# A two-layer decode kernel with 27 unit buffers in place of 26, and 22 kept units of each row in place of 20

## The chip, the cores and the metric

The kernel runs on one core of a Trainium2 chip. The metric is the device time of one execution in microseconds, the median of several. The profile is one further execution; its span, from the first to the last instruction, is 1 to 2 us shorter than the device time.

## The reference

Eight sequences (rows), one new token each, pass through two rounds of attention and MLP. Both rounds use the same weights and the same caches, so a layer-1 query reads the same keys and values as the layer-0 query of its row.

```python
def _A_ref(x, k_cache, v_cache, wq, wo):      # x: 8 x 1 x 640, caches: 8 x 32 x 4096 x 128
    W = min(4096, max(256, Sk // 4))          # the last 1024 positions
    q = (x @ wq) as 32 heads of 128
    k, v = k_cache[:, :, Sk - W:], v_cache[:, :, Sk - W:]
    p = softmax(q k^T * Dh ** -0.5)
    return (p v as 4096 columns) @ wo
def _B_ref(x, w1, b1, w2, b2):                # 640 -> 1728 -> 640
    y = layernorm(x)
    return gelu(y @ w1 + b1) @ w2 + b2
x = x + _A_ref(layernorm(x), ...)             # layer 0
x = x + _B_ref(layernorm(x), ...)
x = x + _A_ref(layernorm(x), ...)             # layer 1
x = x + _B_ref(layernorm(x), ...)
```

All tensors are bfloat16. The used part of the caches is 134 MB[...]; weights are another 15 MB.

## The kernel before

**Units.** A unit is the keys, or the values, of one pair of heads of one row: 128 partitions x 2048 bf16, 512 KB, fetched by one DMA from the SyncE queue (`load`, L357). A row has 16 pairs, so 32 units. `NUNIT = 26` unit buffers hold them. A buffer is free again when the last matmul on it is done (`release`).

**Stream and keep.** In layer 0 each row reads all its 32 units. Pairs 6 to 15 (KEEP, three jobs of 2, 4 and 4 pairs) stay in their 20 buffers until layer 1 of the same row has used them; pairs 0 to 5 (STREAM, two jobs "a" and "b" of 3 pairs) are read and dropped, and read again for layer 1. While a row's 20 kept units wait for its layer-1 query, 6 buffers are left for streams.

**A job** is a set of pairs of one row and layer. Its steps, with the engine and the line in the profile: `expand` puts the queries into a weight with zeros around them (VectorE, L367); `scores`, four matmuls of 512 columns for each unit of keys, on four column groups of the array (TensorE, L377); `exponent` (ScalarE, L386) into the row `p`; `turn`, four small matmuls that transpose p (L392); `place` copies the result among zeros into a `pv` buffer (ScalarE, L400); `totals` and `inverse` give the softmax sums (L405, L409, L411); `values`, four matmuls for each unit of values (L419), into an `o` bank of PSUM; `fold` (four times, L431 and L433) and `halve` (twice, L441 and L443) bring the wanted blocks together in `acc` and `parts`; `gathered` (L448) turns them into columns; `finish` (L475) scales them. In layer 0 `project` (L488) multiplies with wo into the attention bank of PSUM, 5 matmuls of one column for each head, in groups of 15 or 20. In layer 1 `finish` writes the output into the SBUF table `qo`, and all rows are projected together at the end (`gather`, L676). The last job of a row's layer 0 takes values unit by unit into columns (`columns`, L459) in place of values, fold and gather.

**The chain of a row.** When all projections of row b are done, `chain` runs the first MLP for that row alone: add (L608), layer norm (L247 to L272, its root on GpSimd, L264), `hidden` (14 chunks of w1, L300), bias and tanh, `gate` (L317), `outer` (14 chunks of w2, L329), another layer norm, and then the queries of layer 1 (`query`, L619; L623 copies those that are not used at once into `qo`). During this chain the queue streams the jobs of `WINDOWS[b]`: pairs that layer 0 of later rows and layer 1 of earlier rows need. As layer 1 of row b releases its kept units, the kept units of row b + 1 are loaded.

**Order.** Loads stand in a fixed list (`add_loads`): keys of a job and values of the job before it by turns. All instructions of all engines are emitted in the order of the string `ORDER`, which picks at each step one of the tasks left, and which was found by a search over planned durations (the second argument of `plan.add`). `Plan` checks counts of shared things: unit buffers, 2 score banks `s`, 3 query buffers `qz`, 1 row `p`, 2 buffers `pv`, 2 banks `o`, 1 pair `acc` and `parts` (`f`), 3 small banks `c`, 5 `rd`. The waits themselves are put in by the framework from what each instruction reads and writes; it keeps engines apart in a PSUM bank.

**Ends.** The first 20 us or so load wq; the queries of layer 0 for all rows come from one set of matmuls (L667). After the last loads the closing MLP runs for all eight rows together (L742 to the output's DMA at L747).

Of the kernel before, what the change touches and what calls it, by code (L numbers as in the profile page):

```python
# [14 lines left out]
P = 128  # L15
NB = 8
# [9 lines left out]
NFC = 14  # L26
# [3 lines left out]
NUNIT = 26  # L30
STREAM = ((0, 3), (3, 6))
KEEP = ((6, 8), (8, 12), (12, 16))
ALSO = {}
NOT = {}
WINDOWS = ("0:1a 0:1b 0:2a 0:2b", "1:0a 0:3a 0:3b", "1:0b 1:1a 0:4a 0:4b", "1:1b 0:5a 0:5b", "1:2a 1:2b 0:6a 0:6b", "1:3a 1:3b 0:7a 0:7b", "1:4a 1:4b", "1:5a 1:5b 1:6a 1:7a 1:6b 1:7b",)
WINDOWS = [[(int(w[0]), int(w[2]), ord(w[3]) - 97) for w in x.split()] for x in WINDOWS]
WPOS = (("w1", -1), ("w2", -1), ("wo", 8))
NPV = 2
ORDER = (
    ",,)%)y}y}&%y{y{y{+%z/2364/zkzkzkytzjz)z)zh&zgysyuyuysytytzazaz5y}y}y}y}y}y}yt4ysysys&**,*-{ez#{d&3yj),-&+&*{Yy"  # L40
    "hytytzBz@z@yc+z%z%z<+z$z$&ydy`y`ym&&&z1z4z1z3%##{<yuyuyuyuy[y[y[y[y[y[y[y[#{/y^y`y^y_yjy_y_y_{8yvyZy]$y[y[y[y["
    "yWyXy[yWyiyZyZyZyZyZyZyZyXyXz}##$zizizizjyUyUyZyUyUyUyTyTyTyTyTyTyTyTyT%zfzfySySzdzuySySyYzTyTzSz^yT#zQyRzYz[%"
    "yTyTzX#zLzL#yOyOyOyOyOyOyOzXyOzJzKzUzCyOzByOyOz%zOzDz%z`z%yiz$yizIzIz#zHz8z8yi#yhyhyOyOz,yfyfz/#z.yvz/yNyN;yMy"
    "M-z)z)ypypypz%z%z%yzy{y{##zI4yxy[y[z0y~yIyjytyuyuywyw($.zKygygygygygyWyWyWydydydydyFyVyVyeyFybybyUyayaya###yRy"
    "eyey]y]y]yCysysysyYyZ*&yXyXyOyOyOyOyOyhyAyg%)ygye%%yPymycyNyJ1)yHyHyHy{yHyzyz#yYy9yXyXyXyXy9yWy9##y7yAy7y@yBy@"
    "yQy7yM##ycyJyJyJyJy5#y4y4y4y4y4$%*y@y1yRy3y3y=y3y3y3y3#&##zay-y4z_(yDy3y5yBy5y3y4y?y3y-z|y-zRy<y<zPy-y0#%#y7y-"
    "y-y-y-y-zUy-zDzDzDzFzPy-y-zDy/%y,z?y-y,y,zZy,y,z:y,y,y,#%z5y*y*y*y*y*y*#y$y2y$z3zFy&y&z1y*zBy&y&z.z.z.#y&z#z#z"
    "#z#z*y%y)z4z4z4z(%&y&y#y#y#y#y#yuyuz+y#y#y#y#y#z%z#yp#ypy|%x}yoySymymySyuySySyjyjyj6yix}x}+%#xzycyLxzxzyJxzy1x"
    "zy0y0yYy0y0yZyZyZyZyayWyVyXyXxw$#-yRxtyKyKyPy+y=y?y+y<y<y<y+y+y:y[y[y:y@y:y:xuxuxuy>$y@y@xtxt&+$#y:xp,xoxyxoxo"
    "y*y*y*xwxxy(xwxo(-%&y7xrx|y5xkxkxky2x{x}y0x}.###xkzoxgxgxixgxgxg(($zQxcxcxcxyxhxhxwxwxwxcxcxhzExt#xsxsxgxbz?z?"  # L50
    "#$x`xc#z:z:xbzGxvxvxvxvxvz4xvxk$xa#x`x`x`x`x`x`xbz5z*xbxbx`x`x`x`x`x`x`xbxbxbz(xc$z6xa%x^x_x_#x]x]yox]x^ykx]x]"
    "x]x]ygx]z#x]x]ydx]ykyzycx]ybx]ygyayfys#%&xYx]xYxYxYxVyWy^yhx]xXy[(xW$xVyUy`y`xWyTz(xV$y^#xTyYyZxTxTxTxTyVyaxTx"
    "TxTxTy]y]xUxUyFxUyMyAyAxUy@xRy?xTxTxT2#yByByByByBxdxdxdy?y?y4y4/y4y4y4y9-)06+#xKxK$xJy)xXxLxLx~xVxVxixVxVxVxfx"
    "yxVxVxWxWxbxbxbxWxWy@xVxsxmxmxHx^xkxkxkxIxlxjx}x]xjx]xIxSxSxSxSxIxc&$xPxPxPxRx~%x}xQxO%xixE$y1xgxDxDxDxDxDxDxO"
    "x`xny&xny%xOx_x_x`x`#xh%(%x@xBx@xAxAxAxAx?z/xExCxmx?$x>#.%#*((#x6x8xDz1x8x^xCx7xBxBxAxAxAxDxDxAxEylxEykxCxPyix"
    "6x@x6x6x6x6###x3x9x3x7xCx7x3x6x@yVx@yUydydx6x3#$x3x3yOy]y]x:%x2x2x2x2yVx5x2x2x2x2yFx2x2yBx2x3y@x2x2x2x2x2yUy;x"
    "2&x1x1x1yOyOx1x1x1yL#y;x0yIx1y0(yFx0yEy.x3x/y,y,y,x/x/#y>x/y,y-x.x.x.x.y#y&#x-x-&x~x,#y.%x{xxx*x*x*y%xuxux[y#x"
    "[1*$*#xVxVx>xU%x=xhxhxhxhxhxhx=xRx=xixex=x$xOx_xQx<xbxbx<xixix$x$xg7.%3x6x6x6xWxTxnxVxDxDxTxTxRx8xVw|xNxNw|xAw"
    "yw{xKx2w{x1x1x1xIxIxBxBxBxFx:z,#xPx@&,xAx7x7x7x7x7-ww#wvxC#yvyvxBx2xUys%.x&z$x3x3x&x&x&x-x-x&x&wsyfx%wuydx$xEw"
    "qwtxCx/x/y]x#x$wqw}w~w~w~$w}w}w}wpwp(#$#&wx##$whyRwh#wgwo#yMwowfwfwfwnwnwnwfwfwfwiwiwiwiwiwqwhy/y;wpwpy.whwhwh"  # L60
    "whwhwhy&wjwjwhwiwj#wgwhwhwgwgxwwgwhwgwgwgxrwgwgy-wewfwfwfwfxk$#y$y$xpxpxp##wbxo#wawdxlxcwawawax`y(waxdxdxm$wdx"
    "bw`x[x[wbxZxexexew`waxXxb%xb&##w[w[w[x[xQw[w[w[xWwZxaxMxTxMwZwZwZx1x1xHxHxHwZxT#>,((x+wnx@x@x*x*wnwnwnx5wnx%wn"
    "wnx1x1x#x#x3x#wUwUw}x8w}&wkwkwkx3%x(xUx(x(x(wSwSx,x,x,whxL##x*wQw}w}x&wQx%wQw{wcw~w~w~w~w}wzw|w|$$$*x4x4wxwMx2"
    "w^w^xCwuwwwpwpwhwhwhwhwhwhwkw^w^wlwfw^w^+3/wJwewJwLwsw^+(wpwJwoyUyUw]w]wTwT%yPwjwSwSwiwSwhwhwgwI/*wdwdwdwdy-wS"
    "wSwSwQ.#wCy%y%y%y%w]wCw[w[w[w[wN#%##(##w<y%wGwGwEwOxnwOwFwEwEwLxixiwLwLwEwEwEwEwHwE##$xj#$w@w7xuxZxYxd%w6w6w6w"
    "6w6xSw:w:w:w<w9w9w9w9w9w9w9w:w9w9w6w8w8w8xJw6xV#xHw6#w5w5w5w4w>x8#xKw3xJ#$%w0w3x:w3x0x0w0x/x/x>w0x.x.w0w0w0w0x"
    "-w0xFx,w0w0xCw0w0x&w0x#x>w0w0w0w0w|w|x8x&x&x&#x&w0w0wy#w~x@w/wvw{w/x*w/wZw/w/x%w@wpwWwowow@w@w@w@w@wjw@w/##+2-"
    ".)*w&wGw&wFw)w4wZwYxCwYw)w)w2w2$&&-wQwQwQwKwKwKwNw.wMwMwMw/w/vw#w#wmvw+wXwFw4w4w+wT)*&)&&%$#w;wrwrw7w7w*wGw6mm"
    "rmmm#$ukuwJw;uwHtlllll%kukw0w=w2w0w;w1%#jjjihhhw&hhw$w-w-w-w/w-w$w$w$w$w*w*w$w$w(w&w1iw#w#w.w#w#w#hxCxCvvw(w(v"
    "vviiiiiirp#oopofngggkkfjkjjjjjw{#$dgdfx+%eewrcx%ddg#w}w}cwlccwjwj#bffwh%&c#%wc^^^wi^wh^wg^^wg^wfwdwX]wX]]]^^wR"  # L70
    "wZ^wY^^^^wMwJ^^mwG^wFl+$#-wdwA.w@w@w@$YYw=w=WXXaaaaarw=XXXXX*#kVV$#S##),$)#MMw&]M#NNNllllKkkkVjff#UUvvUJKbrJJJ"
    "^^RIk[[OPw&IIIIKbI#%##o#EEEDDKhhhUI$HCCFE`NNCDDDDDDwwVVXXXG%FSSSFCEEOwgECDDDDDCHHGGCCBwWBBwUBweBBBBB#wNw^w^wN#"
    "$?wY%>AA>CwEwGwG>>>w^@@&==wXwH====wS=#wQwBw7w8<<w5<==#w1w1w7w9<<<<<w,w,w,<).$-.GrGG]t]#$%%$22w&@444232e:22b222"
    "24_]Wff4VE#11VURRwY[#wX000$NUuNNN^NN)%##9---#*D*3*MM*@?o*0H02VF****,*+#MM**))))))#*Sk4**(#((&&&&*,,Z55ZW*+%)%0"
    "0%PM&&&&&&)%3#&1&&$>...%$$8#*+00+####%#(##%#$##")


class Job:


    def __init__(self, b, layer, i0, i1, held, at):
        self.b, self.layer, self.i0, self.i1, self.n = b, layer, i0, i1, i1 - i0
        self.held, self.at, self.loads, self.o8, self.q_ps = held, at, {}, None, None

# [52 lines left out]
def _kernel(ctx: ExitStack, tc: tile.TileContext, A_small, A_k, A_v, A_wq, A_wo, B_w1, B_w2, out):  # L137
# [7 lines left out]
    small = ctx.enter_context(tc.tile_pool(name="small", bufs=2))  # L145
# [4 lines left out]

    units = [unitp.tile([P, UNIT], BF16, name=f"unit{i}") for i in range(NUNIT)]
    wq_sb = wpool.tile([P, NKC, H * DH], BF16, name="wq_sb")
    wo_sb = wpool.tile([P, H, D], BF16, name="wo_sb")
    w2_sb = wpool.tile([P, NFC, D], BF16, name="w2_sb")
    w1_sb = wpool.tile([P, NKC, F], BF16, name="w1_sb")
    in_sb = units[NUNIT - 1][:, 0:NKC * NB + NFC + NKC]

# [4 lines left out]
    ident = const.tile([P, P], BF16, name="ident")  # L162
    make_identity(nc, ident[:])
    cst = const.tile([P, 8], FP32, name="cst")
    ones_f, nhalf, mask, ones_b = cst[:, 0:1], cst[:, 1:2], cst[:, 2:6], cst[:, 6:7].bitcast(BF16)[:, 0:1]
# [3 lines left out]
    nc.vector.tensor_reduce(out=mask, in_=ident[:].rearrange("p (x t) -> p t x", t=4), axis=AX.X, op=ALU.add)  # L169
    sel_f = units[NUNIT - 2][:, 0:16].bitcast(FP32).rearrange("p (i u) -> p i u", u=2)  # L170
    for u in range(2):
        nc.vector.tensor_reduce(out=sel_f[:, :, u], in_=ident[:, 64 * u:64 * u + 64].rearrange(
            "p (h r i t) -> p r i h t", h=2, r=2, i=4)[:, 0], axis=AX.XY, op=ALU.add)
    sel = const.tile([P, 4, 2], BF16, name="sel")
    b2T = const.tile([P, NKC], FP32, name="b2T")
    nc.vector.tensor_copy(sel[:], sel_f)
# [9 lines left out]
    xT = state.tile([P, NKC, NB], FP32, name="xT")  # L186
    b1T = state.tile([P, NFC], FP32, name="b1T")
    qo = state.tile([P, NB, H], BF16, name="qo")
    qzs = [state.tile([P, 2, 4, 4], BF16, name=f"qz{g}") for g in range(3)]
    pvs = [state.tile([P, 4 * 68], BF16, name=f"pv{g}") for g in range(NPV)]  # L190
    xn = state.tile([P, NKC, 1], BF16, name="xn")
    xa = state.tile([P, 2, NKC + 1, 1], FP32, name="xa")
    xb = state.tile([P, NKC, 1], FP32, name="xb")
    xm = state.tile([P, 2, NKC + 1, 1], FP32, name="xm")

    def epsilon(x2, twice):
        nc.vector.memset(x2[:, 0, NKC], 0.0)
        nc.vector.memset(x2[:, 1, NKC], (EPS * EPS if twice else EPS) * D / P)

    epsilon(xa, True)  # L200
    epsilon(xm, False)
    for t in qzs + pvs:
        nc.vector.memset(t[:], 0.0)

    rds = [state.tile([P, 4, 2], FP32, name=f"rd{i}") for i in range(5)]
    ots = [state.tile([P, 8], BF16, name=f"ot{i}") for i in range(2)]

    def bank(*dims):
        t = c_banks.pop(0)
        n = 1  # L210
        for d in dims:
            n *= d
        v = t[:, 0:n]
        if len(dims) == 2:
            v = v.rearrange("p (a b) -> p a b", b=dims[1])
        elif len(dims) == 3:
# [69 lines left out]
    def mlp(step, x2, xbv, nb, dst):  # L286
# [7 lines left out]
        def hidden(k, f0, f1):  # L294
            if f0 == halves[k][0]:
                t["h", k] = bank(NFC // 2, nb)
# [489 lines left out]
```

## Time and profile before

| | before |
|---|---|
| device time, median of 3 | 502.8 us (502.73 to 503.06) |
| span of the profile | 501.2 us |
| read from HBM | 199.56 MB, 398 GB/s over the span |
| unit loads | 176 of keys, 176 of values, 512 KB each |
| time from issue to landing | 8.6 us (keys), 9.8 us (values), median |
| TensorE, VectorE, ScalarE busy | 79%, 42%, 13% |
| mean granted TensorE clock | 0.702 |

A load's time from issue to landing is long because several are queued; at most 8 are under way. TensorE's busy time is modelled for overlapping matmuls, so 79% is not 79% of its peak. The clock of the first 130 us has no record in the trace and is shown as 1.00 there. The chain that ended last is 40% DMA and 31% TensorE: the two hand over to each other, a load waiting for a buffer and a matmul for a load.

### The profile page before, as it was taken

How to read it: one execution, taken by the hardware profiler on the slowest of the kernel's cores; microseconds unless marked ns; L12 is line 12 of the kernel's file. 1: busy time of each engine (PE TensorE's matmuls, PEld its weight loads, DVE VectorE, ACT ScalarE, POOL GpSimd, SP SyncE). 2: the span in 40 equal slices, each digit the busy share in tenths (PEclk: the TensorE clock that was granted, in tenths of full speed). 3: DMA queues.
4: the chain of work that ended last, by engine and by line, in shares of the span. 5: the costliest groups of instructions: out<-in, count | busy, mean ns of one | idle time of the engine just before them, and what ended most of it. 6: DMA issues, size and time to landing. Idle time of an engine off the chain costs nothing.

```text
span 501.2 us, 16498 instructions
## 1 busy us (share of the span) xinstructions
PE 396.7 (79%) x7186; PEld 214.6 (43%) x7186; DVE 208.8 (42%) x982; ACT 67.3 (13%) x196; POOL 12.7 (3%) x24
## 2 busy tenths in 40 slices
PE   0442336987889988988799888998899899999984
PEld 0310114543255435543454455433654365356454
DVE  3001032325535353426444554354435634643672
ACT  1010010111101120012101111111112110201210
POOL 1000000000000000000000000000000000000001
PEclk9999999999855576556855675557558555665675
DMA  8999999999999999999999999999999999999980
GB/s 326 419 419 419 432 429 417 416 419 418 416 408 388 415 415 419 417 416 419 417 409 412 419 418 406 401 419 416 417 414 417 417 403 409 417 412 395 414 350 3
DMA packets 52199, 200.63 MB, mean 400 GB/s; under 512 B 6048, under 2 KB 6048, under 8 KB 51104
## 3 DMA queue, kind: packets, MB, share of 16 engines
q1 hardware_dynamic: 52128, 199.59, 98.2%
q8 instruction: 56, 0.92, 0.7%
q14 instruction: 15, 0.12, 0.1%
HBM read 199.56 MB, written 0.01 MB: 398 GB/s over the span
## 4 chain that ended last, share of the span: by engine, by line
DMA 40%; PE 31%; DVE 4%; issue 1%; ACT 1%; POOL 1%; POOLq 0%; SPq 0%; DVEq 0%; ACTq 0%
DMA unit<-in_A_k_dram 21%; DMA unit<-in_A_v_dram 19%; PE s_ps L377 10%; PE o_ps L419 8%; PE c_ps L619 5%; PE att L488 2%; PE c_ps L329 2%; PE c_ps L300 1%; DVE acc L433 1%; PE c_ps L392 1%; PE c_ps L251 1%; PE c_ps L448 1%; PE c_ps L405 1%; PE o_ps L459 1%; POOL ln_w L264 1%
## 5 line engine op out<-in xcount | busy, mean ns | idle before, releaser
L377 PE MATMUL s_ps<-unit,qz 128*4 128x512 bf16 x1024 | 129.7, 559 | 36.2 <-DMA unit<-in_A_k_dram 29.3
L419 PE MATMUL o_ps<-unit,pv 128*16 128x512 bf16 x884 | 114.5, 558 | 6.8 <-DMA unit<-in_A_v_dram 3.2
L433 DVE SCALAR_TENSOR_TENSOR acc<-o_ps,cst,acc 128x128 f32<-128x128 f32 x213 | 74.0, 348 | 5.7
L386 ACT ACTIVATE p<-s_ps 128x512 bf16<-128x512 f32 x80 | 47.8, 598 | 207.3 <-PE s_ps L377 190.1
L377 PEld LDWEIGHTS <-qz 128*4 128x4 bf16 x1024 | 24.2, 89 | 64.3 <-issue 48.4
L488 PEld LDWEIGHTS <-wo_sb 128*128 128x128 bf16 x1280 | 38.8, 102 | 24.5 <-issue 19.1
L488 PE MATMUL att<-ot,wo_sb 128*128 128x1 bf16 x1280 | 42.2, 165 | 7.3 <-DMA wo_sb<-in_A_wo_dram 4.5
L619 PEld LDWEIGHTS <-wq_sb 128*128 128x128 bf16 x1280 | 37.9, 103 | 22.0 <-issue 21.7
L431 DVE TENSOR_SCALAR acc<-o_ps,cst 128x128 f32<-128x128 f32 x71 | 24.4, 343 | 53.2 <-PE o_ps L419 52.2
L619 PE MATMUL c_ps<-xn,wq_sb 128*128 128x1 bf16 x1280 | 40.7, 165 | 1.1 <-DVE xn L272 0.8
L409 DVE TENSOR_REDUCE rd<-c_ps 128x6 f32<-128x48 f32 (+2 forms) x80 | 16.4, 205 | 49.2 <-PE c_ps L405 35.3
L400 ACT CAST pv<-c_ps 128x48 bf16<-128x48 f32 (+2 forms) x80 | 16.1, 202 | 147.2 <-PE c_ps L392 109.5
L419 PEld LDWEIGHTS <-pv 128*16 128x16 bf16 x884 | 22.5, 96 | 29.3 <-issue 18.8
L448 PEld LDWEIGHTS <-parts 128*128 128x128 bf16 x142 | 11.2, 103 | 40.8 <-DVE parts L441 16.8
L448 PE MATMUL c_ps<-sel,parts 128*128 128x8 bf16 x142 | 18.3, 176 | 12.9 <-DVE parts L441 8.2
L392 PEld LDWEIGHTS <-p 128*128 128x128 bf16 x320 | 14.8, 104 | 30.3 <-issue 16.9
L392 PE MATMUL c_ps<-ident,p 128*128 128x16 bf16 x320 | 21.2, 176 | 5.5 <-ACT p L386 4.1
L459 PE MATMUL o_ps<-pv,unit 128*128 128x1 bf16 x560 | 19.1, 165 | 7.2 <-DMA unit<-in_A_v_dram 6.2
L300 PEld LDWEIGHTS <-w_sb 128*128 128x128 bf16 x630 | 18.9, 104 | 10.7 <-issue 10.7
L329 PEld LDWEIGHTS <-w_sb 128*128 128x128 bf16 x630 | 18.6, 104 | 7.7 <-issue 7.5
L459 PEld LDWEIGHTS <-unit 128*128 128x128 bf16 x560 | 17.2, 102 | 10.9 <-DMA unit<-in_A_v_dram 7.7
L443 DVE TENSOR_TENSOR parts<-acc,parts 128x128 bf16<-128x128 f32 x71 | 20.4, 287 | 1.9
(85 smaller groups left out, 225.1 us busy)
## 6 DMA issues: line engine op xcount, KB each, us to landing
unit<-in_A_v_dram SPq DMA_DIRECT2D x176, 512.0 KB, 9.8
unit<-in_A_k_dram SPq DMA_DIRECT2D x176, 512.0 KB, 8.6
wq_sb<-in_A_wq_dram SPq DMA_DIRECT2D x5, 1024.0 KB, 9.1
wo_sb<-in_A_wo_dram SPq DMA_DIRECT2D x1, 5120.0 KB, 20.8
w_sb<-in_B_w_dram SPq DMA_DIRECT2D x1, 2240.0 KB, 28.8
w_sb<-in_B_w_dram SPq DMA_DIRECT2D x1, 2160.0 KB, 24.7
unit<-in_A_small_dram SPq DMA_DIRECT2D x1, 14.8 KB, 1.7
out_dram<-unit SPq DMA_DIRECT2D x1, 10.0 KB, 1.4
```

Source lines behind the costliest of these rows:

```text
L300: nc.tensor.matmul(t["h", k][1][:, fc - halves[k][0], :], lhsT=w1_sb[:, kc, c0:c0 + P], rhs=t["y"][:, kc, :], start=(kc == 0), stop=(kc == ...
L329: nc.tensor.matmul(t["o"][1][:, n, :], lhsT=w2_sb[:, fc, n * P:(n + 1) * P], rhs=t["g", k][:, fc - halves[k][0], :], start=(fc == 0 and n ...
L377: nc.tensor.matmul(job.s_ps[32 * a:32 * a + 4, :], lhsT=job.qz[:, a // 2, i - job.i0, :], rhs=k[:, 512 * a:512 * a + 512], start=(i == job ...
L386: nc.scalar.activation(job.p[:], job.s_ps[:], ACT.Exp, scale=QSCALE)
L392: nc.tensor.matmul(job.t_ps[1][:, c], lhsT=job.p[:, c * P:(c + 1) * P], rhs=ident[:].rearrange("p (a r) -> p a r", a=4)[:, :, 0:4], start= ...
L419: nc.tensor.matmul(job.o_ps[32 * g:32 * g + 16, :], lhsT=job.pv[:, i - job.i0, g], rhs=v[:, 512 * g:512 * g + 512], start=(i == job.i0), s ...
L431: nc.vector.tensor_scalar(out=job.acc[:], in0=o[:, 0], scalar1=mask[:, 0:1], scalar2=None, op0=ALU.mult)
L433: nc.vector.scalar_tensor_tensor(out=job.acc[:], in0=o[:, t], scalar=mask[:, t:t + 1], in1=job.acc[:], op0=ALU.mult, op1=ALU.add)
L448: nc.tensor.matmul(job.o8[1], lhsT=job.parts[:, h], rhs=sel[:].rearrange("p i u -> p (i u)"), start=(h == 0), stop=(h == 1))
L459: nc.tensor.matmul(job.o_ps[:, h:h + 1], lhsT=v[:, c * DH:(c + 1) * DH], rhs=job.pd[:, i - job.i0, g, t:t + 1], start=(first and c == 0), ...
L488: nc.tensor.matmul(att_bank[:, c:c + 1], lhsT=wo_sb[:, h, n * P:(n + 1) * P], rhs=job.ot[:, h - 2 * job.i0:h - 2 * job.i0 + 1], start=open ...
L619: nc.tensor.matmul(job.q_ps[1][:, h - 2 * job.i0:h - 2 * job.i0 + 1], lhsT=wq_sb[:, kc, h * DH:(h + 1) * DH], rhs=xn[:, kc, :], start=(kc ...
```

## The change

Two pairs' worth of room is made in SBUF for one more buffer, and each row keeps pairs 5 to 15 (22 units) instead of 6 to 15 (20 units), so that layer 1 reads 5 pairs again in place of 6. The room comes from small tables: the constants and per-row vectors are packed into two tiles (`low`, `misc`), with the query and `pv` patterns laid so that tables lie between their zeros; `qo` moves into the PSUM bank that the projections use, with a late copy `qs` in the dead part of wq for `gather`; the residual x moves there too, put in by an identity matmul; `p`, `acc` and `parts` share one row `scr`; and the last 64 rows of w2 are folded into 3 blocks of 128 columns in place of 5. STREAM job "b" has 2 pairs, the first KEEP job 3. `ORDER` is replaced.

```diff
-NFC = 14
+NFC = 15
-NUNIT = 26
-STREAM = ((0, 3), (3, 6))
-KEEP = ((6, 8), (8, 12), (12, 16))
+NUNIT = 27
+STREAM = ((0, 3), (3, 5))
+KEEP = ((5, 8), (8, 12), (12, 16))
-NPV = 2
...
+    low = const.tile([P, 176], BF16, name="low")
+    w_sb = wpool.tile([P, NKC * F + NHC * D + 3 * P], BF16, name="w_sb")
+    w1_sb, w2_sb = w_sb[:, 0:NKC * F], w_sb[:, NKC * F:]
+    scr = state.tile([P, 512], BF16, name="scr")
+    misc = state.tile([P, 304], BF16, name="misc")
...
+    acc, parts = scr[:, 0:256].bitcast(FP32), scr[:, 256:512].rearrange("p (h d) -> p h d", h=2)
...
-    qo = state.tile([P, NB, H], BF16, name="qo")
-    qzs = [state.tile([P, 2, 4, 4], BF16, name=f"qz{g}") for g in range(3)]
-    pvs = [state.tile([P, 4 * 68], BF16, name=f"pv{g}") for g in range(NPV)]
+    qo = att_bank[:, 128:128 + NB * H].rearrange("p (b h) -> p b h", b=NB)
+    qs = wq_sb[:, 0, 24 * DH:24 * DH + NB * H].rearrange("p (b h) -> p b h", b=NB)
+    own = att_bank[:, 0:NKC * NB].rearrange("p (b k) -> p b k", b=NB)
+    final = att_bank[:, NKC * NB:2 * NKC * NB].rearrange("p (k b) -> p k b", b=NB)
+    nc.tensor.matmul(own, lhsT=ident, rhs=x0.rearrange("p k b -> p b k"), start=True, stop=False,
+                     skip_group_check=True)
...
@@ hidden
-                c0 = min(fc * P, F - P)
+                c0 = fc * P if fc <= NHC else F - P
@@ gate
+            pieces = [(slice(0, P), slice(0, n))]
+            if k == 1:
...
+                pieces += [(slice(HALF * i, HALF * i + HALF), slice(n + i, n + i + 1)) for i in range(2)]
@@ outer
-            for fc in range(f0, f1):
+            for fc in range(f0, min(f1, NHC)):
...
+            if f1 == NFC:
+                g = t["g", k][:, 6:8, :]
+                for n in range(0, NKC, 2):
+                    m = min(2, NKC - n)
+                    nc.tensor.matmul(t["o"][1][:, n:n + m, :], lhsT=w2_sb[:, NHC * D + n * P // 2:NHC * D + n * P // 2 + P],
+                                     rhs=g[:, 0:m, :], start=False, stop=True, skip_group_check=True)
@@ scores
-            nc.tensor.matmul(job.s_ps[32 * a:32 * a + 4, :], lhsT=job.qz[:, a // 2, i - job.i0, :],
+            nc.tensor.matmul(job.s_ps[32 * a:32 * a + r + 1, :],
+                             lhsT=view(low, job.qz + 5 + d - (d + 1) * r, (d + 1, r + 1)),
@@ exponent
-        nc.scalar.activation(job.p[:], job.s_ps[:], ACT.Exp, scale=QSCALE)
+        nc.scalar.activation(scr[:], job.s_ps[:], ACT.Exp, scale=QSCALE)
@@ values
-            nc.tensor.matmul(job.o_ps[32 * g:32 * g + 16, :],
-                             lhsT=job.pv[:, i - job.i0, g],
+            nc.tensor.matmul(job.o_ps[32 * g:32 * g + 4 * r + 4, :], lhsT=view(misc, 48 * r + g, (4, 4 * r + 4)),
@@ finish, layer 1
-            dst = qo[:, job.b, 2 * i0:2 * i1]
+            dst = (qs if job.direct else qo)[:, job.b, 2 * i0:2 * i1]
...
-    plan = Plan({"unit": NUNIT, "s": 2, "qz": 3, "p": 1, "pv": NPV, "o": 2, "f": 1, "ot": 2, "c": 3, "rd": 5})
+    plan = Plan({"unit": NUNIT, "s": 2, "qz": 3, "p": 1, "pv": 1, "o": 2, "ot": 2, "c": 3, "rd": 4})
...
@@ fold, first; gathered gives it back
-                last = plan.add(DVE, 0.37, lambda k=k: fold(job, k), after=[last], rank=r1, take="f" if k == 0 else None,
+                last = plan.add(DVE, 0.37, lambda k=k: fold(job, k), after=[last], rank=r1, take="p" if k == 0 else None,
...
@@ before gather
+    def move(b0, b1, h0, h1):
+        nc.vector.tensor_copy(qs[:, b0:b1, h0:h1], qo[:, b0:b1, h0:h1])
```

## The prediction

> **What bounds the kernel now.** I read the page first: busy shares, then the 40 slices, then the DMA queue.
>
> ```profile
> PE 396.7 (79%) x7186; PEld 214.6 (43%) x7186; DVE 208.8 (42%) x982; ACT 67.3 (13%) x196; POOL 12.7 (3%) x24
> PE   0442336987889988988799888998899899999984
> ...
> PEclk9999999999855576556855675557558555665675
> DMA  8999999999999999999999999999999999999980
> GB/s 326 419 419 419 432 429 417 416 419 418 416 408 388 415 415 419 417 416 419 417 409 412 419 418 406 401 419 416 417 414 417 417 403 409 417 412 395 414 350 3
> q1 hardware_dynamic: 52128, 199.59, 98.2%
> ```
>
> DMA moves 199.6 MB and is level at about 418 GB/s in nearly every slice, so bytes set most of the time; it dips only in a few slices (388, 401 to 409, 395). TensorE is not far behind: 8 to 9 tenths in every slice after the seventh. So fewer bytes help until one of two things bites: the queue runs short of free buffers, or TensorE has no time left. The waits of the queue that issues the loads show that buffers already matter:
>
> ```profile
> SPq L357 <- DMA unit<-in_A_k_dram: 90.4, 111, 4.0
> SPq L357 <- PE o_ps L419: 71.1, 82, 2.7
> SPq L357 <- PE s_ps L377: 69.0, 86, 4.1
> SPq L357 <- DMA unit<-in_A_v_dram: 67.0, 89, 2.2
> ```
>
> The two DMA rows mean that the queue is full (it waits for an older load); the two PE rows, 140 us together, mean that the next buffer is still being read. To place them I cut the run where the last kept unit of a row lands and where the first layer-1 query is ready ("held": all 20 kept units occupied, 26 - 20 = 6 buffers left for streams), and between ("open"):
>
> ```profile
> 140.00:160.00 20.00, 17.71 (x367) 11.48 (x363) 8.93 (x46) 2.01 (x7) 1.08 (x2) 0.50 1.01 398
> 160.00:188.00 28.00, 25.75 (x410) 11.49 (x408) 13.48 (x60) 5.29 (x15) 0.00 (x0) 0.61 1.02 412
> 188.00:211.00 23.00, 20.14 (x430) 13.36 (x433) 8.46 (x47) 2.08 (x7) 1.09 (x2) 0.59 1.03 417
> 244.00:264.00 20.00, 17.18 (x367) 11.57 (x367) 6.97 (x38) 1.78 (x6) 1.08 (x2) 0.57 1.03 410
> 292.00:315.00 23.00, 20.06 (x433) 13.37 (x433) 10.03 (x53) 2.62 (x8) 1.08 (x2) 0.63 1.02 406
> 349.00:371.00 22.00, 19.51 (x388) 12.48 (x385) 9.62 (x50) 2.72 (x8) 1.08 (x2) 0.50 1.03 417
> 405.00:417.00 12.00, 11.79 (x259) 7.97 (x259) 4.03 (x25) 1.90 (x6) 1.08 (x2) 0.50 1.01 397
> 446.00:460.00 14.00, 13.25 (x268) 8.47 (x264) 4.89 (x29) 1.90 (x6) 1.08 (x2) 0.50 1.02 400
> 460.00:482.00 22.00, 21.05 (x373) 10.13 (x370) 13.56 (x59) 4.72 (x14) 0.00 (x0) 0.73 1.02 411
> ```
>
> (Columns: stretch, length, busy and count of PE, weight load, DVE, ACT, POOL, clock, DMA share, GB/s.) Seven held stretches, rows 1 to 7, 134 us in all; weighted by length they run at 408 GB/s against 418. In row 0's the queue is busy with the weights. How many loads are then under way follows from time to landing times rate: loads issued at 150 to 160, at 250 to 260 and at 470 to 480 us,
>
> ```profile
> unit<-in_A_k_dram SPq DMA_DIRECT2D x4, 512.0 KB, 5.7
> ```
>
> ```profile
> unit<-in_A_v_dram SPq DMA_DIRECT2D x6, 512.0 KB, 6.8
> ```
>
> ```profile
> unit<-in_A_v_dram SPq DMA_DIRECT2D x6, 512.0 KB, 9.9
> ```
>
> give 5.8 us (mean with the V row's 5.8) x 389 GB/s / 524 KB = 4.3 loads; 6.8 x 411 / 524 = 5.3; 9.9 x 416 / 524 = 7.9. So of six free buffers about five are in flight and one is being read, and the rate falls from 418 to 389 as loads in flight go to 4.3. That is my price for a lost buffer.
>
> [...] the granted clock is 0.50 or 1.00 and the shortest score matmul takes 376 ns against a median of 587. [...] In this trace the attention bank is shared by few: only L608 waits for it, 5.9 us over 8 times. [...] here 14.8 KB took 1.7 us to land. [...]
>
> **The change, part by part.**
>
> Loads. Layer 0 reads all 32 units of each of 8 rows (256); layer 1 re-reads what isn't kept: 6 pairs x 2 x 8 = 96, together the page's 176 + 176. After: 5 x 2 x 8 = 80, so 16 loads fewer, 8.39 MB; at 418 GB/s 1.254 us each, 20.1 us. The packed w2 saves 64 KB, 0.2 us. The saved loads are the third pair of each layer-1 job "b": by WINDOWS five of them (10 loads, 12.5 us) come before row 7's kept units have landed, three (6 loads, 7.5 us) in the last window.
>
> Free buffers while held: 27 - 22 = 5 in place of 6. With one load less in flight the held stretches go from about 5.1 (their mean rate 408) to 4.1. The line through 389 at 4.3 and 411 at 5.3 gives 385 at 4.1: 134 us x 408 / 385 = 142, so +7.9 us. Bounds: half as much if the reader is served sooner (398 GB/s, +3.3); and if the landing time does not fall below the 5.8 us seen, 4.1 x 524 / 5.8 = 370 GB/s, +13.6. I take 7.9.
>
> The last window (446 to 490). The 6 loads saved there are 7.5 us of DMA, but the layer-1 arithmetic is the same: 32 units of row 7, kept or streamed. TensorE is busy 13.25 of 14 and 21.05 of 22 us, and 7.11 of the last 8: it has 2.6 us of idle. So at least 2 us come off[...]. I take 4 of 7.5.
>
> Queries and layer-1 outputs move into the attention bank. The project groups (L488, about 72) now share it with 56 expand copies (L367, 0.17 us), some 40 finish writes (L475, 0.16 us) and 16 store copies (L623, 0.16 us). [...] behind a waiting project stand the scores and values of TensorE's queue, and for these waits the loads. Bounds: 0 where all fall in idle time, 72 x (0.16 + 0.1 of hand-over) = 19 us if none does. ORDER puts them in order of planned time, so most are over when asked for, and TensorE is idle 10% anyway: 1.5 us.
>
> One scratch row for p, acc and parts, one pv in place of two. A job uses the row for an exponent and its turn (0.6 + 0.3 us) and then for four folds, two halves and the gather (4 x 0.35 + 0.22 + 0.29 + 0.2, about 2.1): 3 us, 80 times, is 240 us of 480. In the stream the last K lands one load, 1.25 us, before the job-before's last V, so exponent and fold follow each other by themselves; waits elsewhere are hidden by the stream. 0, and the reason for the upper bound above.
>
> MLP. 5 more hidden and 2 fewer outer matmuls at 0.03 us, two more gate pieces at 0.17: +0.5 us in each row's chain, hidden by the stream except row 7's; in the closing MLP, which nothing hides, +0.1 and a memset and two pieces (0.07 + 2 x 0.22), +0.6. Together +1.1. Tables packed, other views, strided weights (4 and 16 columns as before or fewer), the extra set-up before 20 us (behind wq's loads), copies in place of adds, moves of old rows at the end (five or so of 0.2 us, before the last landing): 0.
>
> Sum: -12.5 - 0.2 + 7.9 - 4 + 1.5 + 1.1 = -6.2, so 502.8 - 6.2 = 496.6.
>
> **The rivals.**
>
> All of it is saved: free buffers come sooner because less is streamed, and the last window gets the full clock. For: above five loads in flight the rate is flat, and 188 to 211 keeps 417 GB/s while held. Against: 389 at 4.3. Time 502.8 - 20.3 + 1.1 = 483.6.
>
> Five buffers are too few, and the shared bank, row and pv hold units longer: +13.6 held, +5 for the bank, 1 us off the last window, and 2 us for exponents that wait: -12.7 + 13.6 + 5 - 1 + 2 + 1.1 = +8, 511. For: 140 us of buffer waits already, TensorE 95% busy in held stretches 405 to 417 and 446 to 460. Against: DMA dips only 2.5% there now.
>
> Give and take cancel: 12.7 + 2 against 12 + 1.5 + 1.1, 503.
>
> **How the numbers follow.** Forecast region (488 to 501) 0.54; all saved 0.18; cancels 0.06; slower 0.22. Faster 0.72, same 0.05 and slower 0.23 after rounding. The range reaches to near both outer cases with some 0.1 left out at each end: 485 to 508.
>
> **What would show it.** 168 + 168 unit loads and 191 MB; last landing near 482 (now about 488) with the tail still 13 to 14 us; held stretches at 380 to 390 GB/s with 4 loads in flight and open ones at 416 to 419; TensorE at 9 tenths or more and the clock at 1.00 more often in the last window. Wrong if held stretches stay over 400 (then nearer 484) or fall under 370, or if L488 waits for L367, L475 or L623 by more than 5 us, or p waits long for the folds.

## The result and the profile after

| | before | after |
|---|---|---|
| time, median (range) | 502.88 us (502.73 to 503.06) | 507.06 us (506.68 to 507.82) |
| ratio | 1 | 1.0085, 95% interval 1.0067 to 1.0102 |
| span of the profiled run | 501.2 us | 505.1 us |
| unit loads | 176 + 176 | 168 + 168 |
| last unit lands at | 488.3 us | 490.8 us |

The loads went away as counted, and the kernel became 4.2 us slower. The page of after, the lines that answer to those shown of before:

```profile
PE 400.0 (79%) x7203; PEld 213.9 (42%) x7203; DVE 216.5 (43%) x1002; ACT 74.9 (15%) x196; POOL 12.7 (3%) x24
PE   1412356989798979898998899878999999889984
...
PEclk9999995555955765556555665565555555755765
DMA  8999999999999999999999999999899999998970
GB/s 328 417 420 420 442 421 413 400 412 418 417 349 382 414 417 360 396 419 418 363 357 415 417 378 367 413 417 419 299 359 416 418 345 374 418 354 318 417 296 2
...
q1 hardware_dynamic: 49824, 191.13, 95.5%
```

The best slices carry 417 to 420 GB/s as before, but about one in three falls to 299 to 382, where before dipped to 388 to 409. There are 8.5 MB less to move, worth 20 us at the full rate; the dips take all of it back, and the last unit lands 2.5 us later than before. Most of the loss lies in the held stretches, from the landing of a row's last kept unit until its first kept unit is released. The same windows as in the prediction, for four of after's (stretch, length, busy and count of PE, weight load, DVE, ACT, POOL, clock, DMA share, GB/s):

```profile
140.00:157.00 17.00, 15.82 (x342) 10.64 (x343) 7.25 (x42) 2.21 (x7) 1.08 (x2) 0.50 0.96 363
245.00:262.00 17.00, 16.43 (x369) 10.92 (x365) 7.86 (x41) 2.79 (x8) 1.08 (x2) 0.50 0.94 337
353.00:371.00 18.00, 16.08 (x363) 11.25 (x366) 8.27 (x44) 1.94 (x7) 1.08 (x2) 0.50 0.93 327
448.00:463.00 15.00, 14.33 (x348) 10.23 (x348) 6.01 (x36) 2.01 (x7) 1.08 (x2) 0.50 0.84 308
```

308 to 363, where 385 was forecast. What waits for what is in the view of waits (engine, line, releaser: us in total, times, longest). Line numbers are after's: exponent L424, turn L430, place L434, scores L415, values L456, first fold L464, gathered L480.

```profile
ACT scr L424 <- PE c_ps L480: 127.9, 44, 5.7
ACT scr L424 <- PE s_ps L415: 117.2, 20, 13.7
DVE scr L464 <- PE c_ps L430: 53.9, 40, 3.9
ACT misc L434 <- PE o_ps L456: 40.0, 21, 4.8
```

In before the exponent waited mainly for its own scores, six times for another job's turn, and the first fold for its own values:

```profile
ACT p L386 <- PE s_ps L377: 190.1, 45, 15.2
ACT p L386 <- PE c_ps L392: 15.7, 6, 4.7
DVE acc L431 <- PE o_ps L419: 52.2, 29, 16.8
```

In after 44 of 80 exponents are released by the gather of *another* job, because that job's `acc` and `parts` lie where `p` must go; 40 of 71 first folds are released by another job's turn, for the same reason. The idle time itself costs nothing, ScalarE is 15% busy; it shows who is last. The waits of the queue that issues the loads hardly tell the two kernels apart. Its two TensorE rows are 144.8 us together, against 140.1 in before, and the longest wait, 18.9 us, falls in row 0's chain at 82 us, where before also waits, 14.3 us. The shortage shows in the rate and in the count of loads under way, not here:

```profile
SPq L392 <- DMA unit<-in_A_k_dram: 103.6, 105, 4.7
SPq L392 <- PE s_ps L415: 92.7, 72, 18.9
SPq L392 <- DMA unit<-in_A_v_dram: 61.5, 74, 3.6
SPq L392 <- PE o_ps L456: 52.1, 65, 2.6
```

One round of it, from the timeline of after (start, duration, engine and line; in brackets the idle time before it and who ended it; other lines left out):

```profile
251.55 0.35 DVE L464 TENSOR_SCALAR scr<-o_ps,low 128x128 f32<-128x128 f32 x1
...
251.94 0.35 DVE L466 SCALAR_TENSOR_TENSOR scr<-o_ps,low,scr 128x128 f32<-128x128 f32 x1
252.74 0.17 DVE L328 TENSOR_TENSOR misc<-c_ps,low 128x7 f32<-128x7 f32 x1 [0.45 <-PE c_ps L322]
...
253.74 0.73 DVE L466 SCALAR_TENSOR_TENSOR scr<-o_ps,low,scr 128x128 f32<-128x128 f32 x2
...
255.29 0.59 PE L415 MATMUL s_ps<-unit,low 128*1 128x512 bf16 x4
...
256.14 0.23 DVE L473 CAST scr<-scr 128x128 bf16<-128x128 f32 x1
256.40 0.29 DVE L475 TENSOR_TENSOR scr<-scr 128x128 bf16<-128x128 f32 x1
...
257.71 0.21 PE L480 MATMUL c_ps<-low,scr 128*128 128x8 bf16 x2
...
258.01 0.60 ACT L424 ACTIVATE scr<-s_ps 128x512 bf16<-128x512 f32 x1 [2.34 <-PE c_ps L480]
```

The folds start at 251.55, but the row's MLP (L322 to L369) runs between them on both engines: third fold at 253.74, first half at 256.14, gather at 257.71. The row is taken for 6.4 us. The other job's last scores end at 255.88 and its exponent starts at 258.01, 2.1 us late; behind it stand its turn, its place and its values, whose landed units keep, by my count from the trace, 0.6 to 1.6 of the five free buffers on the mean of a held stretch of rows 1 to 7 (0.5 to 1.3 of six in before).

### The profile page after: what moved, and what is told of

It is laid out like the page before. It is cut to its first block, busy times and chain, and to the rows that moved or that the text cites. A ratio compares the mean times of both kernels' runs of the same rounds, so it can differ in the third digit from the quotient of the medians.

```text
span 505.1 us, 16641 instructions
## 1 busy us (share of the span) xinstructions
PE 400.0 (79%) x7203; PEld 213.9 (42%) x7203; DVE 216.5 (43%) x1002; ACT 74.9 (15%) x196; POOL 12.7 (3%) x24
## 4 chain that ended last, share of the span: by engine, by line
PE 55%; DMA 21%; DVE 14%; ACT 3%; issue 3%; POOL 1%; SPq 1%; POOLq 0%; DVEq 0%; ACTq 0%
PE s_ps L415 15%; PE o_ps L456 13%; DMA unit<-in_A_v_dram 12%; DMA unit<-in_A_k_dram 9%; PE c_ps L646 6%; DVE scr L466 5%; PE att L516 5%; PE c_ps L322 4%; PE c_ps L430 3%; PE c_ps L358 2%; ACT scr L424 2%; PE o_ps L491 2%; PE c_ps L480 2%; DVE scr L464 2%; DVE scr L475 2%
## 5 line engine op out<-in xcount | busy, mean ns | idle before, releaser
L415 PE MATMUL s_ps<-unit,low 128*1 128x512 bf16 (+3 forms) x1024 | 127.2, 570 | 21.3 <-DMA unit<-in_A_k_dram 18.5
L456 PE MATMUL o_ps<-unit,misc 128*12 128x512 bf16 (+3 forms) x888 | 114.5, 564 | 18.1 <-DMA unit<-in_A_v_dram 12.7
L424 ACT ACTIVATE scr<-s_ps 128x512 bf16<-128x512 f32 x80 | 47.8, 598 | 267.3 <-PE c_ps L480 127.9
L466 DVE SCALAR_TENSOR_TENSOR scr<-o_ps,low,scr 128x128 f32<-128x128 f32 x213 | 74.2, 348 | 6.1
L464 DVE TENSOR_SCALAR scr<-o_ps,low 128x128 f32<-128x128 f32 x71 | 24.8, 349 | 68.2 <-PE c_ps L430 53.9
L516 PE MATMUL att<-misc,wo_sb 128*128 128x1 bf16 x1280 | 42.1, 165 | 7.3 <-DVE misc L503 2.9
L516 PEld LDWEIGHTS <-wo_sb 128*128 128x128 bf16 x1280 | 39.3, 103 | 15.8 <-issue 13.3
L415 PEld LDWEIGHTS <-low 128*1 128x1 bf16 (+3 forms) x1024 | 23.7, 93 | 50.4 <-issue 39.1
L646 PE MATMUL c_ps<-low,wq_sb 128*128 128x1 bf16 x1280 | 41.8, 165 | 0.5 <-ACT misc L434 0.4
L456 PEld LDWEIGHTS <-misc 128*12 128x12 bf16 (+3 forms) x888 | 20.5, 93 | 41.5 <-issue 24.8
L480 PEld LDWEIGHTS <-scr 128*128 128x128 bf16 x142 | 12.8, 108 | 55.3 <-DVE scr L473 27.7
L434 ACT CAST misc<-c_ps 128x64 bf16<-128x64 f32 (+2 forms) x80 | 21.8, 272 | 96.5 <-PE o_ps L456 40.0
L480 PE MATMUL c_ps<-low,scr 128*128 128x8 bf16 x142 | 20.9, 181 | 16.5 <-DVE scr L473 10.3
L430 PEld LDWEIGHTS <-scr 128*128 128x128 bf16 x320 | 14.8, 105 | 43.0 <-ACT scr L424 33.6
L430 PE MATMUL c_ps<-misc,scr 128*128 128x16 bf16 x320 | 21.4, 177 | 11.6 <-ACT scr L424 10.1
L405 DVE CAST low<-att 128x6 bf16<-128x6 f32 (+2 forms) x56 | 8.0, 152 | 49.6 <-PE s_ps L415 34.6
L322 PEld LDWEIGHTS <-w_sb 128*128 128x128 bf16 x675 | 20.4, 104 | 16.1 <-issue 16.0
L322 PE MATMUL c_ps<-low,w_sb 128*128 128x1 bf16 x600 | 19.0, 165 | 3.0 <-DVE low L294 2.2
```

The source lines that it names most:

```text
L322: nc.tensor.matmul(t["h", k][1][:, fc - halves[k][0], :], lhsT=w_sb[:, kc * F + c0:kc * F + c0 + P], rhs=t["y"][:, kc, :], start=(kc == 0) ...
L415: nc.tensor.matmul(job.s_ps[32 * a:32 * a + r + 1, :], lhsT=view(low, job.qz + 5 + d - (d + 1) * r, (d + 1, r + 1)), rhs=k[:, 512 * a:512 ...
L424: nc.scalar.activation(scr[:], job.s_ps[:], ACT.Exp, scale=QSCALE)
L430: nc.tensor.matmul(job.t_ps[1][:, c], lhsT=scr[:, c * P:(c + 1) * P], rhs=small_ident.rearrange("p (a r) -> p a r", a=4), start=True, stop ...
L434: nc.scalar.copy(view(misc, 0, (64, job.n), (1, 4), (4, 4)), job.t_ps[1][:, :, :, 0:job.n].rearrange("p t a i -> p i a t"))
L456: nc.tensor.matmul(job.o_ps[32 * g:32 * g + 4 * r + 4, :], lhsT=view(misc, 48 * r + g, (4, 4 * r + 4)), rhs=v[:, 512 * g:512 * g + 512], s ...
```

## The experiments

The first seven kernels leave w2 out: it is not loaded and the MLP's second product takes w1's columns. That frees 17 KB a partition for what is to be tried, and ctl27 is the control with nothing else changed. The order of work is after's in all but col27 and befrow2.

**Is it the buffers, the row and pv, or the bank?**

ctl27:

```diff
-    w_sb = wpool.tile([P, NKC * F + NHC * D + 3 * P], BF16, name="w_sb")
+    w_sb = wpool.tile([P, NKC * F + P], BF16, name="w_sb")
...
-        weights[name] = plan.add(SP, 0.1, lambda: nc.sync.dma_start(dst if name != "wo" else dst[:], src), flow=us)
+        weights[name] = plan.add(SP, 0.1, lambda: name == "w2" or nc.sync.dma_start(dst if name != "wo" else dst[:], src), flow=us)
```

> The changed kernel without the load of w2 (outer multiplies by columns of w1 instead, so the MLP's second product is left out); this makes room for the runs beside it. 2176 KB less to load is 5.3 us at 418 GB/s; both theories expect about 502 us, and the held stretches as in the changed kernel: 3.3 to 4.4 loads in flight, 310 to 370 GB/s.

505.17 us (500.92 to 507.71), ratio to before 1.0037 (1.0021 to 1.0052). That is 1.9 us under after, not 5: by my count row 0's held stretch, which the load of w2 no longer fills, now loses 4.4 us in place of 0.8. The shape is after's: the exponents wait 128.0 us for other jobs' gathers.

u28:

```diff
-NUNIT = 27
+NUNIT = 28
```

> The control with a 28th unit buffer, everything else and the order as they are: 6 free buffers while a row is held. Theory A (the count of free buffers starves the queue): one load more in flight, held stretches near 400 GB/s, so about 15 of the 18 us lost there come back: 487 us. Theory B (units stay longer in their buffers because exponents wait for the shared row and place waits for the one pv): the buffer helps only by part, held stretches at 370 to 385, 493 us or more.

503.47 us (499.86 to 504.7), ratio 1.0005 (0.9987 to 1.0022): 1.7 us, with an interval that touches the control's, for a buffer that the forecast priced at 7.9. The exponent's wait is unmoved:

```profile
ACT scr L425 <- PE c_ps L481: 126.2, 44, 5.7
ACT scr L425 <- PE s_ps L416: 118.3, 20, 13.6
```

The sixth free buffer mostly holds one more landed unit that waits for its turn. By my count from the traces, in the held stretches of rows 1 to 7, landed units that keep a buffer go from 1.3 in the control to 2.1, while loads in flight go from 3.7 to 3.9 only. The number of buffers is not what is short.

split27, a row of its own for `acc` and `parts` and a second `pv` in turn:

```diff
+    fol = state.tile([P, 512], BF16, name="fol")
+    misc2 = state.tile([P, 208], BF16, name="misc2")
-    acc, parts = scr[:, 0:256].bitcast(FP32), scr[:, 256:512].rearrange("p (h d) -> p h d", h=2)
+    acc, parts = fol[:, 0:256].bitcast(FP32), fol[:, 256:512].rearrange("p (h d) -> p h d", h=2)
...
+        job.pvt = pvs.pop(0)
...
```

> The control with 27 buffers, but a row of its own for acc and parts and a second pv, as the kernel before had. The order of instructions is unchanged. Theory A: within 2 us of the control (502). Theory B: a streamed unit is released 1 us sooner after landing in held stretches, 0.6 more loads in flight, 385 GB/s there: 494 us or less.

490.79 us (490.07 to 491.7), ratio 0.9766 (0.9749 to 0.9782), 14.4 us under the control. The waits for gathers are gone from the exponent.

qo27, `qo` back in SBUF:

```diff
-    qo = att_bank[:, 128:128 + NB * H].rearrange("p (b h) -> p b h", b=NB)
+    qo = state.tile([P, NB, H], BF16, name="qo")[:]
```

> The control with 27 buffers and the table qo back in SBUF, out of the bank that the projections write. If waits in that bank are what costs (theory C): 5 us or more under the control. Theories A and B: within 1.5 us of the control.

503.1 us (500.51 to 505.71), ratio 1.0002 (0.9987 to 1.0017): 2.1 us under the control, between what the two sides expected.

**Row or pv, and what a buffer is worth once they are apart**

scr27 is split27 with the own row alone, pv27 with the second `pv` alone, split28 is split27 with `NUNIT = 28`.

> The control's kernel (after without w2) with a row of their own for acc and parts; p keeps its row, pv stays one. Theory row (the exponent waits for another job's fold and gather, 127.9 us of ACT idle in after; splitting row and pv together brought the control from 505.2 to 490.8): nearly all of the gain is here, 491 to 494 us, and the exponent's waits for gathers are gone. Theory pv (the single pv makes place wait for the values of the job before, 40.0 us of ACT idle, and with it everything behind it on ScalarE): 501 to 505.

492.24 us (490.54 to 494.2), ratio 0.979 (0.976 to 0.982), 12.9 us under the control. Its exponents:

```profile
ACT scr L426 <- PE s_ps L417: 191.9, 61, 13.7
```

This is before's line again: they wait for their own scores.

> The control's kernel with a second pv in turn and the one row kept. Theory row: 502 to 506, no better than the control, since the exponent of the next job still waits for the fold. Theory pv: 491 to 495. If the two are one chain that either opens halfway, both this and the run with its own row stand near 497.

504.12 us (500.75 to 505.75), ratio 1.0022 (1.0009 to 1.0034): within the control's interval. The row alone makes the loss; the single `pv` costs nothing that these runs can tell.

> Own row, second pv and 28 unit buffers instead of 27 (six free beside 22 kept ones, without w2). Theory buffers (the number of free buffers limits the transfers once units are released on landing, as they now are): the 10.7 us still lost in held stretches of the split kernel fall by half, 484 to 487 us. Theory no buffers (an extra buffer holds one more landed unit, as in the run with 28 buffers and a shared row): within 1.5 us of the split kernel's 490.8.

484.86 us (482.59 to 485.69), ratio 0.963 (0.96 to 0.9659), 5.9 us under split27. The same buffer that gave 1.7 us with one row gives 5.9 with two: here a buffer counts only when what lies in it is used soon.

**Without folds**

col27, whole computation; every value unit is multiplied column by column, as the last job of a row is already:

```diff
-            fn = (lambda i=i: columns(job, i)) if tail else (lambda i=i: values(job, i))
+            fn = lambda i=i: columns(job, i)
...
-            for k in range(4):
-                last = plan.add(DVE, 0.37, lambda k=k: fold(job, k), after=[last], rank=r1, take="p" if k == 0 else None,
...
```

> The whole computation with w2, 27 buffers: every value unit is multiplied by 16 one-column matmuls straight into a bank's head columns, as the last job of a row is already, so folds, halves and the gather are gone, the row holds p alone, and the holes of misc hold two pv. Theory row: with nothing behind the exponent but its own turn, the units leave about 1 us after landing, and the time falls to 488 to 496 us, below before's 502.9. If TensorE's extra one-column matmuls (16 at 27 ns, 0.43 us a unit, against four 512-column ones at 0.43 us at half clock and 0.21 at full) are what then ends the waits, 497 to 504.

513.18 us (512.53 to 515.51), ratio 1.0214 (1.0188 to 1.0239): a miss. An `o` bank is now kept until `finish`, so the written order no longer fitted, and tasks that found no bank were put off and passed by others. The rate is full in many slices, dips much as after's does, and breaks down late, in the view of slices of the page:

```profile
GB/s 330 418 420 418 441 420 415 388 408 416 418 352 383 417 416 358 366 416 417 399 357 416 416 371 350 416 416 417 349 394 417 374 333 384 416 255 341 416 197 3
```

TensorE is busy as long as in after (400.1 us against 400.0), so the changed order is the likelier cause; that was not separated. The exponents wait for their own scores here (248.6 us, 63 times) and no longer for gathers, so these dips have another cause than the row, and the run neither supports nor refutes the row's price.

**The row in the kernel before**

befrow2 puts `p`, `acc` and `parts` of the kernel before into one row, with 26 buffers and two `pv`:

```diff
-        job.p = small.tile([P, 512], BF16, tag="row", name="p", bufs=1)
+        job.p = scr
...
-            job.acc = small.tile([P, P], FP32, tag="acc", name="acc", bufs=1)
+            job.acc = scr[:, 0:256].bitcast(FP32)
...
```

> The kernel before with its row for p also used for acc and parts, nothing else; tasks that find the row taken are put off in the written order, and others pass them. Theory row: the same wait appears with 26 buffers and two pv, exponents wait for gathers by 80 us or more in all, and the time rises by 7 to 15 us, to 510 to 518. If the row hurts only with five free buffers (a unit held longer matters less with six), it stays within 503 to 506.

564.54 us (563.59 to 566.95), ratio 1.1227 (1.1198 to 1.1256). The waits are the forecast ones, in both directions:

```profile
ACT scr L400 <- PE c_ps L462: 165.7, 43, 13.2
ACT scr L400 <- PE s_ps L391: 86.9, 18, 12.2
DVE scr L445 <- PE c_ps L406: 74.8, 34, 17.1
```

In the held stretches of rows 1 to 7, by my count, 3.1 loads are in flight in place of before's 5.3, and landed units keep 2.9 of the six free buffers in place of 0.7. The direction is right and the size at least four times what I expected. The order was not searched again for one row, tasks were only put off, so how much of the 61 us is the row alone stays open. After's order, searched with one row, keeps its cost to 13 us.

**The whole kernel with an own accumulator**

row27 has w2. Each partition of `acc` takes its value from one of four column groups, so it can be folded in bf16, and the halves and the second gather matmul go (142 VectorE operations less):

```diff
+    acc = state.tile([P, P], BF16, name="acc")
...
+    single["hu0"], single["hu1"], b2T = column(att_bank[:, 80:87]), column(att_bank[:, 87:95]), att_bank[:, 95:100]
...
-        for h in range(2):
-            nc.tensor.matmul(job.o8[1], lhsT=parts[:, h], rhs=sel,
+        nc.tensor.matmul(job.o8[1], lhsT=acc[:], rhs=sel, start=True, stop=True)
```

> The whole computation with w2, 27 buffers and after's order, but acc has its own 256 bytes: it is folded in bf16 (each partition takes its value from one of the four column groups, so nothing is summed), the halves and the second gather matmul are gone, and the bytes come from hu and b2T moved into the attention bank, xb into x2s, b1T in bf16 and the last w2 block in half its width. Theory row: the control without w2 gained 13 us by a row of its own, and w2 cost 1.9 us there, so 493 to 496 us, that is my forecast's 496.6 once the row really costs nothing. If the gain needed the 17 KB or the missing w2 load, 502 or more.

502.9 us (501.11 to 505.18), ratio 0.9993 (0.9979 to 1.0007): 4 us under after, not 12. The waits for gathers are nearly gone, but even the fast slices carry only 408 to 411 GB/s. The layout had moved the unit buffers: the first began at byte 160 of its partition, in every other kernel so far at 512. Two more kernels differ from each other in that place alone. Both are row27 without one of w2's 13 full chunks, to make room. row27c begins its units at byte 1536, row27d 32 bytes further on, and the tiles behind the units move along:

```diff
-    fill = const.tile([P, 64], BF16, name="fill")
+    fill = const.tile([P, 80], BF16, name="fill")
```

> The kernel row27 with its unit buffers moved so that each begins at a multiple of 512 bytes in its partition (first at 1536), as in before, after and every kernel run so far but row27, where the first began at byte 160. To make room it leaves out one of w2's 13 full chunks (not loaded, the twelfth is multiplied twice), 0.16 MB of 191, worth some 0.4 us. Theory place: row27's fast slices carried 408 to 410 GB/s and others' 416 to 419 because of the address; they come back to 416 to 419 and the time falls from 502.9 to 492 to 496 us, under both kernels. Theory else (the bf16 accumulator, PSUM operands, w2): 500 to 504 again, 409 GB/s.

> row27c with the units 32 bytes further on (first at byte 1568), nothing else. Theory place: 408 to 410 GB/s in the fast slices and 500 to 504 us. Theory else: the same as row27c within 1.5 us.

row27c: 494.41 us (492.94 to 494.84), ratio 0.9825 (0.9806 to 0.9844). row27d: 503.63 us (500.69 to 508.0), ratio 1.0008 (0.999 to 1.0026). The slices of row27c, then of row27d:

```profile
GB/s 327 417 419 419 429 433 417 391 406 418 418 414 392 412 418 408 402 418 419 417 382 410 419 412 389 388 418 417 400 378 417 417 351 386 418 348 331 417 317 2
```

```profile
GB/s 327 409 410 411 420 430 410 386 394 408 409 396 386 408 408 400 393 408 409 405 373 384 409 395 351 397 408 408 394 369 409 409 396 389 407 362 330 410 293 3
```

417 to 419 against 408 to 411 in the full slices: the 32 bytes make the 9.2 us. With the units at such an address again, the own accumulator brings after's 507.06 to 494.41, and its held stretches look like this (windows of row27c, columns as above):

```profile
140.00:155.00 15.00, 14.07 (x278) 9.07 (x279) 6.67 (x38) 2.19 (x7) 1.08 (x2) 0.50 1.01 404
241.00:256.00 15.00, 14.27 (x286) 8.94 (x283) 6.73 (x35) 2.10 (x7) 1.08 (x2) 0.50 1.00 394
346.00:360.00 14.00, 13.11 (x272) 8.61 (x272) 6.64 (x37) 2.02 (x7) 1.08 (x2) 0.50 1.00 382
437.00:452.00 15.00, 13.49 (x293) 8.97 (x294) 6.07 (x35) 1.92 (x7) 1.08 (x2) 0.50 0.86 301
```

Row 7's is the exception: its last stretch is as slow as after's. A kernel with the own accumulator, all of w2 and the units on such an address was not run; row27c is that kernel but for 0.16 MB of w2. Two further kernels, row27b (row27 with its units moved) and aft0 (after itself with its units begun at byte 160), gave no time, so what the address does to after's own layout was not measured.

Worked out from the traces, for the held stretches of rows 1 to 7 (loads in flight, landed units that keep a free buffer, and rate are means over them; lost is the time that they took beyond their bytes at 418 GB/s):

| | before | after | scr27 | split28 | row27c |
|---|---|---|---|---|---|
| free buffers | 6 | 5 | 5 | 6 | 5 |
| in flight | 5.3 | 3.7 | 4.1 | 4.9 | 4.1 |
| landed, not released | 0.7 | 1.2 | 0.8 | 1.0 | 0.9 |
| GB/s | 405 | 344 | 377 | 395 | 379 |
| lost, us | 3.5 | 21.1 | 10.5 | 6.1 | 10.0 |

## Why the prediction was wrong

It said faster, 496.6; it became slower, 507.1, just inside the range of 485 to 508 but on the other side of before. By its steps:

- **Loads: right in count, 168 + 168 and 191 MB.** The 20.2 us that they are worth, and 2.5 more, were lost again, so the last unit lands at 490.8 and not near 482. Of these 22.7 us the held stretches of rows 1 to 7 account for 17.6 (21.1 lost against 3.5); where the other 5 come from was not looked for.
- **Free buffers, +7.9: about right.** Where the row does not interfere, scr27 and row27c have the forecast 4.1 loads in flight, at 377 and 379 GB/s (forecast 385), and lose 7.0 (scr27) and 6.5 us (row27c) more than before. In after itself it was 3.7 and 344, under the bound of 370; u28 shows that this excess is not the buffers'.
- **One scratch row, 0: this is the step that failed.** It costs 12.9 us without w2 (scr27 against ctl27) and 12.7 in the kernel with it (row27c against after, the halves' removal included). I wrote that "exponent and fold follow each other by themselves", from the order of landing, and counted a turn of 3 us by summing durations: 240 of 480 us. The trace of before held the answer. From the start of the first fold to the end of the gather a job takes 4.55 us there on the mean, not 2.1, since other work, MLP steps among it, comes between on VectorE and TensorE; from the start of the exponent to the end of the turn 2.69 us, not 0.9. 71 x 4.55 + 80 x 2.69 = 538 us, more than the span of 501. For 151 us `p` was in use at the same time as `acc` and `parts`, which one row cannot hold. In after, squeezed, the sum is still 71 x 3.22 + 80 x 1.39 = 340 us. Both signs that the prediction named for this came, held stretches under 370 and `p` waiting for the folds. And "hidden by the stream" overlooked who stands behind the exponent: the values, and with them landed units in the few free buffers (1.2 in after, 0.8 in scr27).
- **One pv, 0: right** within what the runs can tell (pv27).
- **Attention bank, +1.5: right in size,** 2.1 us by qo27, taken in a kernel that still had the one row. The 0.1 us of hand-over in its bound is what before shows for one turn of engines each way: 0.05 us from the end of `finish` to `project` (146.89 to 146.94), 0.04 from the end of `project` to the add of L608 (147.34 to 147.38). Its sign of being wrong stayed away: `project` (L516 in after) waits 3.7 us in all for the lines named there (L405 and L503 in after), under 5.
- **MLP, +1.1: consistent.** From the last landing to the end of the span it is 14.3 us, 12.9 before. No run took it alone.
- **Last window, -4: not tested alone.** What it counts beyond TensorE's 2.6 us of idle was an estimate of mine that no run shows. It is hidden in after, where 448 to 463 runs at 308 GB/s; the clock in 463 to 485 is 0.73, as in 460 to 482 of before.
- **Two readings of before were a little off,** without weight in the sum: TensorE stands at 7 tenths in two slices after the seventh, and in 405 to 417 it is 98% busy (11.79 of 12 us), not 95%.

With the row at 12.7 in place of 0, the forecast's own sum gives 502.8 - 6.2 + 12.7 = 509.3, against 507.1; and row27c's 494.4 lies near the forecast's 496.6, though not every term of that was tested. The second rival, 511, had the direction right by a wrong split: it gave the exponents 2 us and the buffers 13.6.

## What to carry to other kernels

A buffer that two steps are to share is priced by how long each step holds it in the trace, from its first write to its last read, waits in between included, and not by the sum of the operations' durations. The time in which both are in use at once (151 us here) is what the merge has to move, and it costs where streamed data waits for it (12.9 us, scr27 against ctl27). A wait on an engine that is 15% busy can be dear when streamed data stands behind it, because data that has landed and waits takes away the buffers that keep the transfers going (1.2 landed units, 3.7 loads in flight and 344 GB/s in after; 0.8, 4.1 and 377 in scr27). And a buffer added while something else delays its release only fills up (1.7 us against 5.9).

## What the hardware showed that I had not expected

The place of a DMA's destination in the partition mattered: with the units 32 bytes further on, in 4096-byte packets to each partition, the full rate fell from 417 to 419 down to 408 to 411 GB/s, 2%, and the time rose by 9.2 us. A 4096-byte packet took 159 ns at the median and at the 95th percentile in row27c, 162 and 168 ns in row27d. The tiles behind the units moved by the same 32 bytes; that the packets themselves took longer speaks for the DMA and against the engines' operands, but the two were not moved apart.

The units of row27 began at byte 160 and those of row27d at 1568, and both lost about 2% (408 to 411 GB/s in the full slices); the fast kernels began at 512 and 1536 (417 to 419 in row27c). Why the place costs the packets time was not shown, and no other places were tried.
